# Gated mix of cached attention and a feed-forward layer: K transposed in 32x32 blocks by VectorE, K and V in 64 KB pages, TensorE's program as loops

## The chip, the cores and the metric

One core of one Trainium2 chip runs the whole program. The metric is the device time of one execution in microseconds (us); the time of a version is the median of its runs.

## The reference

One token's row `x` (512 numbers) goes through two branches, and a gate mixes them.

```python
g = sigmoid((x * gate_w).sum(-1))
q = x @ wq                                  # 32 heads of 128
scores = q . k_cache * 128 ** -0.5          # 8 groups of K and V, 4 heads each, 32768 positions
a = (softmax(scores) @ v_cache) @ wo        # wo: 4096 x 512
b = (silu(x @ w_gate) * (x @ w_up)) @ w_down   # 1792 wide
out = g * a + (1 - g) * b
```

All tensors are bf16. `k_cache` and `v_cache` are 8 x 32768 x 128 each, 64 MiB; the weights are 13 MiB more. Every number is used once, for four heads in the case of K and V.

## The kernel before

**Layout.** A group's K or V is 8 MiB. SBUF holds five pages of 32 KB per partition: two for K (`PG_K`), two side by side for V (`PG_V`), and one (`PG_X`) for wq at first and wo at the end. `w_gate` and `w_up` lie in the V pages until V's first load; `w_down` has a tensor of its own (`wd`). A K group is loaded in two halves of 32 KB per partition, a V group in one transfer of 64 KB per partition. With `(p r) d -> p (r d)` a partition gets consecutive positions, so every partition reads one run of HBM.

**Scores.** A score is a sum over the 128 numbers of a position, which stand along a partition's row; TensorE sums over partitions. So K has to be transposed. TensorE does it (`emit_fill`, L397): it takes pairs of bf16 as one fp32 word, and multiplies by an identity, into PSUM (`pst`, two buffers). VectorE copies 128x2048 bf16 at a time from PSUM to `ktT` (L606). Then 16 matmuls with 8 columns each (`emit_scores`, L409) use the transposed K as weights and `qcur` as the moving operand: even and odd numbers of each word have a matmul each. A half group has 8 such units. Units of fills run two ahead of the scores (`LAG`).

**Softmax and V.** VectorE takes the maximum of a half's scores (L611), GpSimd the maximum over partitions (L292), ScalarE the negative bias (L504) and eight exponentials with their sums (L513), into `ET`. With `ET` as weights, 64 matmuls of 512 columns (L450) go over V, in four strips of the array (`32 * c`). ScalarE copies the sums out (L525), and the next turn of the loop reduces them (`emit_reduce`, L435); VectorE keeps them in `oT` (L600).

**Order.** Each engine has its own program; semaphores join them. TensorE's loop (L485) has the eight groups as turns: K in two halves, the reduction of the turn before, V. SP issues all loads in one order: wq, x, gate_w, w_gate, w_up, then per group K half, K half, V, then `wd`, and wo in five pieces (`WO_CUTS`). A K load waits until its half page was transposed one group earlier (L301); a V load waits until V of the group before is used up (L311), the first one until the up projection is done.

**The end.** `emit_end` sums the exponentials with a matmul of ones, reduces the last group, multiplies `w_down` (14 rows) and the first 18 rows of wo as one-row matmuls of 512 columns in four strips (L204), then the last rows of wo in pieces of 128 columns (L216) as they land. `part` (L659) joins the strips; L661 copies the result, and L243 stores it.

Of the kernel before, what the change touches and what calls it, by code (L numbers as in the profile page):

```python
# [4 lines left out]

ACT = mybir.ActivationFunctionType
ALU = mybir.AluOpType
# [6 lines left out]
def bass_gated_mix__gqa_block_cached__swiglu_ffn__decode_kernel(  # L14
# [22 lines left out]
    assert H == 32 and G >= 2  # L37
# [3 lines left out]
    R = 128  # L41
    BLK = 128 * R
    NB = S // BLK
    assert S % BLK == 0 and NB == 2
    NT = NB * R
    PAGE = R * DH
    RPU = 8
    UPP = R // (2 * RPU)
    UPG = NB * UPP
    UW = RPU * 128  # L50
    NKT = 4
    NST = 2
    LAG = 2
    STEP = 16
    WOJ = H * DH // 128
    SCALE = float(DH) ** -0.5
    assert UPG == STEP == 4 * HPG and UPP % NKT == 0 and UPP % NST == 0
    assert KC * H * DH <= PAGE and 2 * KC * F <= PAGE and WOJ * NOUT <= PAGE
    WO_CUTS = [0, 8, 18, 26, 30, 32]
    KW = 1  # L60
    WD_CUT = 8
    WIDE = WO_CUTS[KW + 1]
    OC = NOUT // 128

# [4 lines left out]
    assert RQ * HPG <= 32 and RQ * DH == 512  # L69

    PG_K = (0, 1)
    PG_V = 2
    PG_X = 4
    NPG = 5

    with ExitStack() as es:
# [3 lines left out]
        sem_page = [S_(f"s_page{i}") for i in range(3)]  # L80
        sem_q = S_("s_q")
        sem_f = S_("s_f")
        sem_wo = [S_(f"s_wo{i}") for i in range(len(WO_CUTS) - 1)]
        sem_ld_x = S_("s_ld_x")
        sem_ld_wd = S_("s_ld_wd")
        sem_fill = S_("s_fill")
        sem_sc = S_("s_sc")
        sem_v_free = S_("s_v_free")
        sem_cp = S_("s_cp")
        sem_out = S_("s_out")  # L90
        sem_const = S_("s_const")
        sem_pool = S_("s_pool")
        sem_ident = S_("s_ident")
# [5 lines left out]
        sem_pe_S = S_("s_pe_S")  # L99
        sem_pe_O2 = S_("s_pe_O2")  # L100
        sem_pe_sum = S_("s_pe_sum")
# [4 lines left out]
        sem_dve_t1 = S_("s_dve_t1")  # L106
        sem_dve_tT = S_("s_dve_tT")
        sem_pmax = S_("s_pmax")
        sem_dve_esum2 = S_("s_dve_esum2")
        sem_dve_oT1 = S_("s_dve_oT1")  # L110
        sem_dve_oT2 = S_("s_dve_oT2")
        sem_dve_O2 = S_("s_dve_O2")
        sem_dve_oz = S_("s_dve_oz")
        sem_dve_row = S_("s_dve_row")
        sem_psw = S_("s_psw")
        sem_pe_w = S_("s_pe_w")
        sem_dve_w = S_("s_dve_w")
# [3 lines left out]
        sem_ps0 = S_("s_ps0")  # L121
        sem_acc = S_("s_acc")
        sem_red = S_("s_red")
        sem_rc = S_("s_rc")
        sem_exp = S_("s_exp")
        sem_gtot = S_("s_gtot")
        sem_gmax = S_("s_gmax")

# [3 lines left out]
        x_row = T("x_row", [1, D], BF16)  # L132
        gw_row = T("gw_row", [1, D], BF16)
        ones_bf = T("ones_bf", [1, 2], BF16)
        ones_f = T("ones_f", [128, 128], FP32)
        ident = T("ident", [128, 128], BF16)
        ident_f = T("ident_f", [128, 128], FP32)
        perm = T("perm", [128, 2, 128], BF16)
        pmat = T("pmat", [128, 128], BF16)
        xT = T("xT", [128, KC], BF16)  # L140
        gwT = T("gwT", [128, KC], FP32)
# [6 lines left out]
        qblk = T("qblk", [128, (G + 2) * STEP], BF16)  # L148
        qcur = T("qcur", [128, 2, 2 * HPG], BF16)
        sg = T("sg", [128, FC], FP32)  # L150
        t1 = T("t1", [128, FC], FP32)
        tT = T("tT", [128, FC], BF16)
        wd = T("wd", [128, FC, NOUT], BF16)
        page = T("page", [128, NPG, PAGE], BF16)
        ktT = T("ktT", [128, NKT, 2 * UW], BF16)
        ET = T("ET", [128, NT, HPG], BF16)
        pmaxf = T("pmaxf", [128, NB, HPG], FP32)
        pmax = T("pmax", [128, (G + 1) * STEP], FP32)
        gmax = T("gmax", [128, G, HPG], FP32)
        nbias = T("nbias", [128, G, HPG], FP32)  # L160
        esum = T("esum", [128, G, NB, HPG], FP32)
        esum2 = T("esum2", [128, G, HPG], FP32)
        sel5 = T("sel5", [128, SW + 15], FP32)
        sel4 = sel5[:, SW - 1 : SW + 15]
        acc = T("acc", [128, RQ, DH], FP32)
        oT = T("oT", [128, (G + 2) * STEP], FP32)
        rS = T("rS", [128, H], FP32)
        rSg = T("rSg", [128, H], FP32)
        oTs = T("oTs", [128, H], BF16)
        O2a = T("O2a", [128, WOJ], BF16)  # L170
        O2 = T("O2", [128, WOJ], BF16)
        O2z = T("O2z", [128, WOJ - WIDE, SW], BF16)
        part = T("part", [128, NOUT], FP32)
        res_row = T("res_row", [128, 128], BF16)
# [4 lines left out]
        ps_sc = [P(f"ps_sc{i}", [128, 512], FP32) for i in range(NB)]  # L179
        ps_o = P("ps_o", [128, 512], FP32)  # L180
        ps_m = P("ps_m", [128, 512], FP32)
        pst = [P(f"pst{i}", [128, UW], FP32) for i in range(NST)]
        M_X0 = 0
        M_Q0 = 8
# [3 lines left out]
        M_P0 = M_O0 + WOJ  # L188
        assert M_P0 + HPG <= 512

        ps_e = pst[0][:, 0:512]
        ps_c = pst[1][:, 0:512]
        ps_w = pst[0][:, 512:1024]

        v_page = page[:, PG_V : PG_V + NB, :].rearrange("p b e -> p (b e)")
        v_rows = v_page.rearrange("p (r d) -> p r d", d=DH)

        wq_v = page[:, PG_X, 0 : KC * H * DH].rearrange("p (c n) -> p c n", c=KC)
        wgu = page[:, PG_V, 0 : 2 * KC * F].rearrange("p (w c f) -> p w c f", w=2, c=KC)
        wo_v = page[:, PG_X, 0 : WOJ * NOUT].rearrange("p (j n) -> p j n", j=WOJ)  # L200

        def emit_wide(pe, w, vec, j, first, last):
            c = j % NSTRIP
            return pe.matmul(  # L204
                ps_w[32 * c : 32 * c + 1, :],
                vec[:, j : j + 1],
                w[:, j, :],
                start=first,
                stop=last,
                skip_group_check=True,  # L210
            )

# [13 lines left out]
        def emit_wo(pe, k):  # L226
            pe.wait_ge(sem_wo[k], 16)
            for j in range(WO_CUTS[k], WO_CUTS[k + 1]):
                if j < WIDE:
                    ins = emit_wide(pe, wo_v, O2, j, False, j >= WIDE - NSTRIP)  # L230
                else:
                    ins = emit_rows(
                        pe,
                        lambda e: O2[:, j : j + 1] if e else O2z[:, j - WIDE, :],
                        wo_v[:, j, :],
                        False,
                        j == WOJ - 1,
                    )
            return ins
# [8 lines left out]
        with nc.Block("main") as block:  # L248
            @block.gpsimd
            def _(pool):  # L250
                pool.memset(ones_bf[:, :], 1.0).then_inc(sem_const, 1)
                pool.memset(ones_f[:, :], 1.0).then_inc(sem_const, 1)
# [6 lines left out]

                pool.load_library(library_config.all_libraries[1])  # L260
# [12 lines left out]
                pool.memset(ident[:, :], 0.0)  # L273
                pool.memset(ident_f[:, :], 0.0)
                pool.memset(perm[:, :, :], 0.0)
                pool.memset(sel5[:, :], 0.0)
                chain(pool.memset(pmat[:, :], 0.0))
                ones_where(ident[:, :], 0, [[-1, 128]]).then_inc(sem_ident, 1)
                ones_where(ident_f[:, :], 0, [[-1, 128]]).then_inc(sem_ident, 1)
                for e in range(2):  # L280
                    ones_where(perm[:, e, :], -e, [[0, 2], [-2, 64]]).then_inc(sem_ident, 1)
                ones_where(pmat[:, :], 0, [[-1, 32], [-32, 4]]).then_inc(sem_ident, 1)
                for c in range(NSTRIP):
                    chain(ones_where(sel4, -32 * c, [[-1, 16]]))
                pool.sem_inc(sem_ident, 1)
# [4 lines left out]
                for g in range(G):  # L290
                    pool.wait_ge(sem_pmax, STEP * (g + 1))
                    pool.partition_all_reduce(  # L292
                        gmax[:, g, :], pmax[:, g * STEP : g * STEP + HPG], 128, ReduceOp.max
                    ).then_inc(sem_gmax, 1)

            @block.sync
            def _(sp):
                def load_k(g, b):
                    if g:
                        sp.wait_ge(sem_fill, UPG * (g - 1) + UPP * (b + 1))  # L300
                    sp.dma_start(  # L301
                        page[:, PG_K[b], :],
                        A_k_cache[0, g, :, :].rearrange("(p b r) d -> b p (r d)", b=NB, r=R)[b],
                    ).then_inc(sem_page[b], 16)

                def load_v(g):
                    if g:
                        sp.wait_ge(sem_v_free, g)
                    else:
                        sp.wait_ge(sem_pe_h, 1)  # L310
                    sp.dma_start(  # L311
                        v_page, A_v_cache[0, g, :, :].rearrange("(p r) d -> p (r d)", r=NT)
                    ).then_inc(sem_page[NB], 16)

                sp.dma_start(wq_v, A_wq.rearrange("(p c) n -> p c n", c=KC)).then_inc(sem_q, 16)
                sp.dma_start(x_row[0:1, :], A_x[0, :, :]).then_inc(sem_ld_x, 16)
                sp.dma_start(gw_row[0:1, :], gate_w.unsqueeze(0)).then_inc(sem_ld_x, 16)
                for w, src in enumerate((B_w_gate, B_w_up)):
                    sp.dma_start(
                        wgu[:, w, :, :], src.rearrange("(p c) f -> p c f", c=KC)  # L320
                    ).then_inc(sem_f, 16)
                for g in range(G):
                    for b in range(NB):
                        load_k(g, b)
# [369 lines left out]
```

## Time and profile before

| | us |
|---|---|
| median of 3 runs | 350.92 (350.90 to 350.92) |
| the profiled execution, its own time | 350.87 |
| its span (first to last instruction) | 349.6 |
| PE busy, share of the span | 253.9, 73% |
| DVE busy | 176.0, 50% |
| ACT busy | 33.3, 10% |
| POOL busy | 6.9, 2% |
| granted TensorE clock, mean | 0.883 |

In the profile PE is TensorE's matmuls, PEld its weight loads, DVE VectorE, ACT ScalarE, POOL GpSimd, SP the engine that issues the loads. Busy time of an engine is the union of its instructions. A line such as `L606 DVE COPY ktT<-pst ... x128 | 155.4, 1223 | 115.7 <-PE pst L397 108.1` is a group: source line, engine, operation, what it writes and reads, count, then busy us, mean ns of one, then the us in which the engine stood idle before these instructions, and whose end ended that idle time. A line of the waits has the waiter, the one waited for, us in total, times, and the longest. In the chain that ended last each step is what released the step behind it.

### The profile page before, as it was taken

Reading aid. Unit: us, or ns where it says so; the run is one execution under the profiler, and the core shown is the slowest. Engines: PE = TensorE matmul, PEld = TensorE weight load, DVE = VectorE, ACT = ScalarE, POOL = GpSimd, SP = SyncE. Lnnn points to the kernel's source line nnn. Section 1 sums busy time; section 2 is a strip of 40 time slices with the busy share of each in tenths; the row PEclk is TensorE's granted clock in tenths of the full one; section 3 lists DMA queues with packets and bytes.
Section 4 is the critical chain, followed back from the end, with each engine's and each line's share of the span. In section 5 each row is a group of like instructions: output and inputs, shape, how many; then the busy total and the mean of one; then the engine's idle time right before and its main releaser. Section 6 shows DMA issues by size and latency. Waiting matters only on the chain. (4 is left out here: it accounts for less than half of the span.)

```text
span 349.6 us, 8827 instructions
## 1 busy us (share of the span) xinstructions
PE 253.9 (73%) x4005; PEld 215.2 (62%) x4005; DVE 176.0 (50%) x194; ACT 33.3 (10%) x148; POOL 6.9 (2%) x29
## 2 busy tenths in 40 slices
PE   0446986688945995798955994598866994698584
PEld 0446986278914985298914993298725993398531
DVE  0010986068801984068803883078703883098511
ACT  1000001300030003000030003000030003000210
POOL 4000000000000000000000000000000000000000
PEclk9999999599968997689969987889968987899879
DMA  8999999999989999999999999999999998999995
GB/s 322 419 457 418 472 444 386 428 420 465 457 386 431 442 442 412 432 469 405 442 416 439 457 405 424 435 461 435 405 427 435 457 435 386 450 469 420 391 421 240
DMA packets 4772, 148.23 MB, mean 424 GB/s; under 512 B 538, under 2 KB 540, under 8 KB 796
## 3 DMA queue, kind: packets, MB, share of 16 engines
q1 hardware_dynamic: 4760, 148.12, 98.6%
q8 instruction: 6, 0.10, 0.1%
q14 instruction: 2, 0.02, 0.0%
q10 hardware_dynamic: 4, 0.00, 0.0%
HBM read 148.11 MB, written 0.00 MB: 424 GB/s over the span
## 5 line engine op out<-in xcount | busy, mean ns | idle before, releaser
L606 DVE COPY ktT<-pst 128x2048 bf16<-128x2048 bf16 x128 | 155.4, 1223 | 115.7 <-PE pst L397 108.1
L397 PE MATMUL pst<-ident_f,page 128*128 128x128 f32 x1024 | 144.4, 292 | 28.9 <-DMA page<-in_A_k_cache_dram 24.8
L397 PEld LDWEIGHTS pst<-ident_f,page 128*128 128x128 f32 x1024 | 120.9, 150 | 35.2 <-DMA page<-in_A_k_cache_dram 28.4
L409 PE MATMUL ps_sc<-qcur,ktT 128*128 128x8 bf16 x2048 | 67.6, 166 | 9.0 <-DVE ktT L606 8.0
L409 PEld LDWEIGHTS ps_sc<-qcur,ktT 128*128 128x128 bf16 x2048 | 66.5, 96 | 11.5 <-DVE ktT L606 9.4
L450 PE MATMUL ps_o<-page,ET 128*16 128x512 bf16 x512 | 45.1, 529 | 33.8 <-ACT ET L513 24.8
L450 PEld LDWEIGHTS ps_o<-page,ET 128*16 128x16 bf16 x512 | 15.4, 116 | 60.2 <-ACT ET L513 34.5
L513 ACT ACTIVATE ET<-ps_sc,nbias 128x128 bf16<-128x128 f32 x64 | 23.9, 552 | 0.6
L504 ACT ACTIVATE nbias<-gmax 128x4 f32<-128x4 f32 x8 | 1.6, 205 | 229.7 <-POOL gmax L292 229.7
L513 ACT ACTIVATION_READ_ACCUMULATOR ET<-ps_sc,nbias 128x1 f32 x64 | 18.0, 282 | 0.0
L611 DVE TENSOR_REDUCE pmaxf<-ps_sc 128x4 f32<-128x512 f32 x16 | 11.1, 691 | 11.9 <-PE ps_sc L409 11.9
L383 PE MATMUL ps_m<-xT,page 128*128 128x1 bf16 x112 | 6.9, 198 | 4.9 <-DMA page<-in_B_w_up_dram 4.9
L435 PE MATMUL ps_m<-sel,acc 128*128 128x4 f32 x72 | 10.0, 262 | 0.4 <-ACT acc L525 0.4
L383 PEld LDWEIGHTS ps_m<-xT,page 128*128 128x128 bf16 x112 | 6.8, 163 | 5.0 <-DMA page<-in_B_w_up_dram 5.0
L346 PE MATMUL ps_m<-ones_bf,x_row 1*128 1x1 bf16 x4 | 0.3, 173 | 13.1 <-DMA gw_row<-in_gate_w_dram 13.1
L435 PEld LDWEIGHTS ps_m<-sel,acc 128*128 128x128 f32 x72 | 9.4, 204 | 0.5 <-ACT acc L525 0.5
L525 ACT ACTIVATE acc<-ps_o 128x512 f32<-128x512 f32 x8 | 4.8, 597 | 47.3 <-issue 47.3
L292 POOL PARTITION_ALL_REDUCE gmax<-pmax x8 | 3.0, 371 | 311.9 <-DVE pmax L613 311.9
L346 PEld LDWEIGHTS ps_m<-ones_bf,x_row 1*128 1x128 bf16 x4 | 0.2, 116 | 13.1 <-DMA gw_row<-in_gate_w_dram 13.1
L546 DVE CAST xT<-ps_m 128x4 bf16<-128x4 f32 x1 | 0.2, 160 | 12.0 <-PE ps_m L346 12.0
L585 DVE TENSOR_TENSOR t<-sg,ps_m 128x14 f32<-128x14 f32 x1 | 0.2, 169 | 10.7 <-ACT sg L498 10.7
L359 PE MATMUL ps_m<-xT,page 128*128 128x1 bf16 x128 | 3.6, 165 | 0.3 <-DVE gwT L547 0.3
(65 smaller groups left out, 31.0 us busy)
## 6 DMA issues: line engine op xcount, KB each, us to landing
page<-in_A_k_cache_dram SPq DMA_DIRECT2D x16, 4096.0 KB, 27.5
page<-in_A_wq_dram SPq DMA_DIRECT2D x1, 4096.0 KB, 12.5
page<-in_A_wo_dram SPq DMA_DIRECT2D x2, 1024.0 KB, 40.4
page<-in_B_w_gate_dram SPq DMA_DIRECT2D x1, 1792.0 KB, 15.7
page<-in_B_w_up_dram SPq DMA_DIRECT2D x1, 1792.0 KB, 20.6
wd<-in_B_w_down_dram SPq DMA_DIRECT2D x1, 1792.0 KB, 36.1
page<-in_A_wo_dram SPq DMA_DIRECT2D x1, 1280.0 KB, 40.7
page<-in_A_wo_dram SPq DMA_DIRECT2D x1, 512.0 KB, 43.6
```

What stands on the lines that cost most here:

```text
L292: pool.partition_all_reduce(gmax[:, g, :], pmax[:, g * STEP : g * STEP + HPG], 128, ReduceOp.max).then_inc(sem_gmax, 1)
L359: ins = pe.matmul(ps_m[:, M_Q0 + h : M_Q0 + h + 1], wq_v[:, c, h * DH : (h + 1) * DH], xT[:, c : c + 1], start=(c == 0), stop=(c == KC - 1),)
L383: ins = pe.matmul(ps_m[:, base + j : base + j + 1], wgu[:, w, c, :].rearrange("d (p j) -> d j p", j=FC)[:, j, :], xT[:, c : c + 1], start= ...
L397: ins = pe.transpose(pst[u % NST][:, k * 128 : (k + 1) * 128], kv[:, n * 128 : (n + 1) * 128], ident_f[:, :],)
L409: ins = pe.matmul(ps_sc[b][:, col : col + 2 * HPG], kt[:, k, e, :], qcur[:, e, :], start=(e == 0), stop=(e == 1),)
L435: ins = pe.matmul(ps_m[:, M_P0 : M_P0 + HPG], acc[:, q, :], sel4[:, q * HPG : (q + 1) * HPG], start=(q == 0), stop=(q == RQ - 1),)
L450: ins = pe.matmul(ps_o[32 * c : 32 * c + RQ * HPG, :], ET[:, n : n + RQ, :].rearrange("p n h -> p (n h)"), v_rows[:, n : n + RQ, :], start ...
L504: act.activation(nbias[:, g, :], gmax[:, g, :], ACT.Copy, scale=-SCALE).then_inc(sem_nbias, 1)
L513: act.activation(ET[:, b * R : (b + 1) * R, h], sc[:, h, :], ACT.Exp, bias=nbias[:, g, h : h + 1], scale=SCALE, accum_out=esum[:, g, b, h ...
L525: act.activation(acc[:, :, :].rearrange("p q d -> p (q d)"), ps_o[:, :], ACT.Copy).then_inc(sem_acc, STEP)
L606: dve.tensor_copy(ktT[:, u % NKT, :], pst[u % NST][:, :].bitcast(BF16)).then_inc(sem_cp, 1)
L611: dve.tensor_reduce(pmaxf[:, b, :], sc, AX.X, ALU.max).then_inc(sem_pmax, 4)
```

## The change

K and V each come as one transfer per group of 64 KB per partition. SBUF has three pages of 64 KB: K in pages 0 and 1 in turn, V in page 2. wq, `w_gate` and `w_up` lie in page 2 until the first V; `w_down` and wo go to page 0 after the last K that used it.

TensorE no longer transposes K. VectorE does, straight from the page to `slot` (two slots of 2 KB per partition): `dve.transpose` on fp32 words turns every 32x32 block of words, 128x512 words per instruction, 32 instructions per group. A quarter of 32 partitions is transposed by itself, so partition 32 i + b of a slot holds word b of a 32-word stretch of positions of quarter i. `qblk` is laid out to fit: four matmuls (`JE`) per row block, each with 16 columns, 4 heads for each of 4 quarters (before: two matmuls with 8 columns). The sum of matmuls for scores stays 2048. The exponentials come out by quarter (`E`), and ScalarE copies them to `ET` in the order that V's rows have: 16 copies of 32 partitions x 256 per group, after the copy to `acc`.

TensorE's program is written as loops: the q projection (16 turns), gate and up (14), the scores of a group (16 turns of two units), `w_down` (7), and around scores, V and reduction a loop over `G + 2` turns with branches (`hinted`). In turn j stand the scores of group j, V of group j - 1 and its reduction.

```diff
-    R = 128
-    RPU = 8
-    NKT = 4
-    WO_CUTS = [0, 8, 18, 26, 30, 32]
+    RPU = 2
+    SLOTS = 2
+    NPG = 3
+    WO_CUTS = [0, 24, 28, 30, 32]
+    K_PAGES = 2
+    V_PAGE = 2
+    W_PAGE = 2
+    O_PAGE = 0
+    V7_CUTS = [0, 64, 192, 256]
...
             @block.sync
+                def load_k(j):
+                    if j >= K_PAGES:
+                        sp.wait_ge(sem_tr, UNITS * (j - K_PAGES + 1))
+                    cache(A_k_cache, j, j % K_PAGES).then_inc(sem_k[j % K_PAGES], 16)
+                def load_v(j):
+                    if j:
+                        sp.wait_ge(sem_v_done, VTURN * (j + 1))
...
+                load_k(0)
+                for j in range(G - 1):
+                    load_k(j + 1)
+                    load_v(j)
+                sp.wait_ge(sem_tr, UNITS * (G - 1))
+                sp.dma_start(wd_v, ...).then_inc(sem_ld_wd, 16)
+                for k, sem in enumerate(sem_v7):
+                    a, b = V7_CUTS[k], V7_CUTS[k + 1]
+                    sp.wait_ge(sem_v_done, VTURN * (G - 1) + b // (RQ * VB))
+                    cache(A_v_cache, G - 1, V_PAGE, a, b).then_inc(sem, 16)
+                for k in range(len(sem_wo)):
...
             @block.tensor
-                def emit_fill(b, u):
...
+                def emit_s(j):
+                    n0 = pe.compute_val(j * UNITS)
+                    c0 = pe.compute_val((j & 1) * (RB * NS))
+                    with pe.Fori(0, UNITS // SLOTS, 1) as u:
+                        for s in range(SLOTS):
+                            pe.wait_ge(sem_tr, n0 + u * SLOTS + (s + 1))
+                            for r in range(RPU):
+                                for e in range(JE):
+                                    ins = pe.matmul(ps_sc[...], sv[:, s, r, e // 2, e % 2, :],
+                                                    qcur[:, e, :], ...)
+                            ins.then_inc(sem_sc, 1)
+                def emit_v(j):
+                    pe.wait_ge(sem_v, j * 16)
+                    pe.wait_ge(sem_ep, j)
+                    pe.wait_ge(sem_oc, j)
...
+                def emit_reduce(n):
+                    pe.wait_ge(sem_acc, n)
+                    for q in range(RQ):
+                        ins = pe.transpose(ps_o[:, q * 128 : (q + 1) * 128],
+                                           acc[:, q * 128 : (q + 1) * 128], ident_f[:, :])
+                    ins.then_inc(sem_red, 1)
...
+                def emit_wide():
+                    with pe.Fori(0, FC // 2, 1) as n:
+                        for c in range(2):
+                            pe.matmul(ps_w[0:1, :], vec[:, bass.ds(n * 2 + c, 1)], page[...], ...)
...
+                with hinted(pe, "groups", G + 2) as (j, arm):
+                    with pe.If(j < G + 1):
+                        arm()
+                    with pe.If(j < G):
+                        emit_s(j)
+                    with pe.If(j > G):
+                        emit_wide()
+                    with pe.Else():
+                        with pe.If(j > 0):
+                            emit_v(j)
+                        emit_reduce(j + 1)
...
             @block.scalar
+                    act.wait_ge(sem_v_done, j * VTURN + VTURN)
+                    act.activation(acc[:, :], ps_o[:, :], ACT.Copy).then_inc(sem_acc, 1)
+                    act.wait_ge(sem_exp, j * HPG + 3 * HPG)
+                    for g in range(NQ):
+                        for i in range(NQ):
+                            ins = act.activation(ET[QP * i : ..., ...], E[QP * g : ..., ...], ACT.Copy)
+                    ins.then_inc(sem_ep, 1)
...
             @block.vector
-                            dve.tensor_copy(ktT[:, u % NKT, :], pst[u % NST][:, :].bitcast(BF16))
...
+                        for t in range(UNITS):
+                            s = t % SLOTS
+                            dve.wait_ge(sem_sc, n0 + (t + 1))
+                            dve.transpose(slot_f[...], kp[:, :, t * UW : (t + 1) * UW]...)
+                                .then_inc(sem_tr, 1)
+                        dve.wait_ge(sem_sc, n0 + (UNITS + SLOTS))
+                        dve.tensor_reduce(pmax[:, :], ps_sc[...], AX.X, ALU.max).then_inc(sem_pmax, 1)
+                        dve.tensor_copy(qc, qblk[...])
+                        dve.wait_ge(sem_red, i * K_PAGES + (p + 1))
+                        dve.tensor_reduce(oT[...], o_diag, AX.XY, ALU.add).then_inc(sem_oc, 1)
```

The sums of the exponentials are taken over partitions by GpSimd (`partition_all_reduce` of `esum`) in place of TensorE's matmul with ones; some constants are filled by GpSimd in place of VectorE.

## The prediction

> **What bounds the kernel now.** I read the DMA part of the page first, then the chain of work that ended last, then SP's waits.
>
> ```profile
> q1 hardware_dynamic: 4760, 148.12, 98.6%
> ...
> HBM read 148.11 MB, written 0.00 MB: 424 GB/s over the span
> ```
>
> The 16 DMA engines are busy 98.6% of the span: the load of 148 MB is the kernel. The chain's last pieces (start, length, what) say it again:
>
> ```profile
> 303.85 43.69 DMA page<-in_A_wo_dram
> 347.53 0.04 issue
> 347.57 0.32 PE pst L216 x4
> 347.90 0.02 issue
> 347.92 0.29 DVE res_row L661
> ```
>
> The last piece of wo was issued at 303.85 us, long before its turn, and 2.0 us after it lands (347.53) the span ends. SP never runs dry, although it waits for pages:
>
> ```profile
> SPq L301 <- PE pst L397: 176.7, 14, 14.9
> SPq L311 <- PE ps_o L450: 87.4, 7, 14.7
> ```
>
> These waits cost nothing: a K load is issued 27.5 us (median) before it lands and a V load 32.1 us, so a backlog stands in the queue. The trace's landings: two K parts take 9.71 us each, a V group 19.35 us. The work on the engines is hidden under that, so taking it away is worth nothing by itself. What counts is (a) the bytes per second, (b) whether a load is ever issued too late, (c) what remains after the last landing.
>
> **Part 1, the transfers.** The bytes are the same. K goes in 64 KB per partition, as V does now: 19.35 for 19.42 us, 8 x 0.07 = **-0.6 us**. wo in 24, 4, 2, 2 rows takes what it took in five pieces (9.96 us). Six fetches of instructions, 16 KB each, hold one DMA engine 1 us each today; fewer of them is at most 6 us on 16 engines, 0.4 us, left out.
>
> **Part 2, K's transpose moves from TensorE to VectorE.** Gone: 1024 matmuls of L397 and 128 copies of L606, both hidden under DMA now. New: 256 transposes of 128x512 words. The nearest rows (lines of VectorE; busy, mean ns):
>
> ```profile
> L611 DVE TENSOR_REDUCE pmaxf<-ps_sc 128x4 f32<-128x512 f32 x16 | 11.1, 691 | 11.9 <-PE ps_sc L409 11.9
> L600 DVE COPY oT<-ps_m 128x4 f32 (+1 forms) x9 | 1.5, 162 | 1.4 <-PE ps_m L435 1.4
> ...
> L640 DVE STREAM_TRANSPOSE O2a<-oTs 128x32 bf16<-128x32 bf16 x1 | 0.2, 211 | 0.0
> ```
>
> A column costs (691-162)/508 = 1.04 ns, so a transpose of 512 words is 211 + 480 x 1.04 = 0.71 us. Two copies of 1.22 us that waited for nothing took 2.35 us together, so back to back an instruction costs 0.09 less: 0.62. Bounds: a copy of 2048 bf16 costs 0.6 ns per element, which would give 0.50 (0.41 spaced); two cycles per word would give 1.21. I take 0.62, by the row of the same operation.
>
> There are two slots, so transpose t waits until the scores have read slot t-2. That round trip stands in this stretch of the timeline (start, length):
>
> ```profile
> 324.83 2.54 DVE L606 COPY ktT<-pst 128x2048 bf16<-128x2048 bf16 x2
> ...
> 327.42 0.56 PE L409 MATMUL ps_sc<-qcur,ktT 128*128 128x8 bf16 x16 [0.54 <-DVE ktT L606]
> ...
> 328.08 0.69 DVE L611 TENSOR_REDUCE pmaxf<-ps_sc 128x4 f32<-128x512 f32 x1 [0.72 <-PE ps_sc L409]
> ```
>
> From the copy's end (327.37) through 16 matmuls to VectorE's next start is 0.71 us; a unit now has 8 matmuls, at 0.025 us each 0.2 less: 0.51. Two units need 0.71 + 0.51 = 1.22 us, as much as 2 x 0.62. TensorE's new loop has a branch every two units: the loop's edge at L485 took 0.40 us in the trace's records, some 0.1 of it in the round trip. So a unit is about **0.65 us** (0.61 to 0.80: doubled matmul times or an edge of 0.7 us give the upper end), and the scores S of a group take 31 x 0.65 + 0.71 + 0.5 = 21.4 us.
>
> **Part 3, is a load late?** One V page instead of an early fill: V(j+1) may be issued only when V(j) is used up. TensorE does the scores of j+1 and then V(j); VectorE, at a group's end, waits for the reduction that follows V(j-1), and all its transposes of the next group are queued behind that. So one turn is S 21.4 + V 5.4 + acc copy 0.6 (L525) + four transposes 0.8 (L397) + a reduce 0.25 + semaphores 0.2 = 28.7 us, against 38.7 us of DMA per group. In the **middle** nothing is late. ScalarE's 16 new copies per group (each between 0.20, L504, and 0.60, L525: 3 to 10 us) run beside S and are due after it: no cost while they stay under 20 us. The matmul loops at the start (30 edges of 0.4 us more) end near 37 us, and K's first group lands at 42.4: hidden, with 5 us to spare. GpSimd's sums and fills lie beside loads.
>
> **At the start:** scores of group 0 from 42.4 to 63.9; then maximum (1.22), GpSimd and bias (0.8), four exponentials (2.1), acc, transposes, reduce: 6 us; scores of group 1 from 69.9 to 91.3; V(0) until 95 to 97; V(1)'s first packet 1 us later (the first load took 0.74 to 1.74). K(2) fills DMA until 100. Hidden with 2 us to spare: it is lost from a unit of 0.69 us on, with 64 us per us of unit.
>
> **At the end** the cover is thin. SP's order is K7, V6, wd (4.3 us), V7 in three parts, wo. The first part of V7 waits for the first 64 rows of V6 to be used, and wo is queued behind it. K7 lands at x; scores until x + 21.5 (V6 landed at x + 19.35); 16 matmuls, the semaphore, SP and first packet: x + 23.7 to 24.6. wd's packets end at x + 23.1. **+1.0 us** (0.6 to 1.5), growing 32 us per us of unit.
>
> **Part 4, after the last landing.** Today wo lands after V by 14 us, which hides V, sums and wd. Now V7's last part is followed only by wo, 9.95 us; from its landing T to the end of the last matmuls that DMA alone would allow is T + 10.3. The chain: 16 matmuls, 1.1 to 2.0; acc 0.65; four transposes 0.7 to 1.05; branches 0.2; 14 matmuls of wd, now all in one strip, so one after the other, 14 x 0.216 = 3.0 (4.7 with the first eight at 0.427); O2 0.6; then 24 wide matmuls not before wo's first piece (T + 7.5) 1.5; copy of part 0.75 (L659); rows 0.45 + 0.65. It ends at T + 10.8 to 12.2: **+0.5 to +1.9**, I take 1.2.
>
> The spread is TensorE's clock, seen in the two stretches of one V stage (the last three columns: granted clock, DMA share, GB/s):
>
> ```profile
> 97.60:104.30 6.70, 3.59 (x36) 1.34 (x40) 0.00 (x0) 2.54 (x16) 0.00 (x0) 0.50 0.91 391
> 104.40:110.00 5.60, 1.72 (x32) 0.59 (x24) 0.00 (x0) 0.60 (x1) 0.00 (x0) 1.00 1.06 456
> ```
>
> Four matmuls side by side took 0.427 us at clock 0.5 and 0.216 at 1.0. [...]
>
> **Sum**, against the profiled execution: span 349.6 - 0.6 + 1.0 + 1.2 = 351.2; its own time, 350.87, is 1.27 over its span: 352.5. The median of the runs is 350.92, the same within 0.05. **Forecast 352.5 us**, +0.45%.
>
> **Rivals.**
> 1. *Nothing is late.* If VectorE keeps 0.61 us per unit and the clock stays at 1.0, the gap at the end is 0.2 or nothing and the tail 0.4 or less: 349.6 - 0.6 + 0.0 to 0.6 + 1.27 = 350.3 to 350.9, not slower. For it: the 2 us of margin everywhere else, and a clock of 1.0 in half of the windows. Against: wd in one strip. It decides below a unit of 0.62.
> 2. *The round trip is the pace.* At 0.80 us per unit, start and end both starve: (0.80 - 0.69) x 64 = 7.0, and 1.0 + 0.15 x 32 = 5.8: 349.0 + 12.8 + 1.2 + 1.27 = 364. For it: only two slots, a branch per two units. Against: the 0.51 us of the trace.
> 3. *Words transpose at half rate*: 1.21 us, S 39.6, a turn of 47 us beats DMA's 38.7 in all groups: the first V is used up at about 133 us, the sixth after at 133 + 6 x 47 = 415, then V7 19.4, wo 10, 2: about 445. The only transpose in the trace is of bf16.
> 4. *TensorE's code is not at hand.* The final branch to the second block waits for a 16 KB fetch (in the trace's records 1 us to a first packet, 1 us of packet, 0.5 us to landing): 2.5 us in the tail, 355.0. [...] The trace's branch at L485 shows no such stall (0.40 us).
>
> That K's path stays on TensorE is ruled out: no instruction of L397 is left.
>
> **How the numbers follow.** Forecast (with gaps of 0.5 to 4 us in all) 0.44; rival 4 0.03; rival 1 0.25; rival 2 and units between 0.69 and 0.85 0.22; rival 3 0.06. Range 350.2 to 362: it leaves out rival 3, the top of 2, and the lowest part of 1. A difference of 0.2% (350.2 to 351.6) is about what this measurement can tell from none. Faster, 0.12, is half of rival 1, with fewer fetches beside; same, 0.23, its other half and the forecast's low edge; slower, 0.65, the rest. The forecast's own range is 351 to 355.
>
> **What would show it.** Transposes near 0.71 us each, spaced 0.65; DMA share again near 0.98 with its only dips at V7's first part; V7's first issue after wd's end by a us; the last matmuls 1 us behind wo's landing. A K group that lands later than 19.35 us after the load before it, anywhere in the middle, would make the prediction wrong, as would transposes over 0.9 us.

## The result and the profile after

379.85 us is the median (379.57 to 381.08, 4 runs) against 350.92 before in the same runs: a ratio of 1.083 (95% interval 1.081 to 1.086). The forecast was 352.5, in a range to 362. The profiled execution of the changed kernel has a span of 379.6 us, 30.0 more than before.

The page after, its row of DMA by slices of the span, its queue and its rate:

```profile
DMA  8999997987903999999999999999989999978993
...
q1 hardware_dynamic: 3752, 148.12, 91.2%
q8 instruction: 1, 0.02, 0.0%
...
HBM read 148.11 MB, written 0.00 MB: 390 GB/s over the span
```

The bytes are the same; the 16 DMA engines are busy 91.2% of the span instead of 98.6%. The row says where not: from the seventh to the thirteenth slice (57 to 123 us; the zero alone is 9.5 us without a transfer) and from the 36th on (332 us). In between nearly all is 9. SP's waits say on whom the loads waited:

```profile
SPq L314 <- PE ps_o L446: 256.6, 9, 39.4
SPq L314 <- PE ps_m L399: 56.8, 1, 56.8
...
SPq L314 <- DVE slot L625: 22.8, 1, 22.8
```

Before, SP's waits for pages came to 290 us (336 now) and cost nothing, since a backlog stood in the queue. Now one wait of 56.8 us, for the up projection (`ps_m`, L399), holds V(0) until 60.6 us. Before, the same load left SP at 29.74, after this wait:

```profile
SPq L311 <- PE ps_m L383: 26.0, 1, 26.0
```

The landings (when a load's last part has arrived, by the semaphore) give the loss at each place, as the time from one landing to the next beyond the usual 19.35 us:

| load | landed after (us) | late by |
|---|---|---|
| K(0), K(1) | 40.96, 60.31 | 0 |
| V(0) | 83.01 | 3.35 |
| K(2) | 105.54 | 3.18 |
| V(1) | 142.71 | 17.81 |
| K(3) to V(6), `w_down` | 340.69 | 0.2 in all |
| V(7) in three parts | 364.53 | 4.48 |
| wo, last piece | 374.42 | 0 |
| end of the span | 379.6 | 5.2 behind wo, before 2.0: 3.2 |

Together 32.2. Some came back: K takes 0.31 less in the first group and 7 x 0.08 after it, and 1.17 at the start, where the up projection lands at 21.61 instead of 22.78. That leaves 30.2 for the 30.0 by which the span grew.

The timeline of the changed kernel shows what the first wait waits for (start, length, what):

```profile
57.91 1.14 PE L399 MATMUL ps_m<-xT,page 128*128 128x1 bf16 x8 [0.40 <-issue]
...
59.44 1.14 PE L399 MATMUL ps_m<-xT,page 128*128 128x1 bf16 x8 [0.40 <-issue]
60.62 0.33 SPq L314 DMA_DIRECT2D page<-in_A_v_cache_dram  x1
...
61.71 1.30 DVE L625 STREAM_TRANSPOSE slot<-page 128x512 f32<-128x512 f32 x2 [0.36 <-issue]
```

A turn of the gate and up loop takes 1.54 us for 8 matmuls of one column, and idle time is put down to "issue": TensorE waits for nothing but its own program. The last turn ends at 60.6, and both V(0)'s load and the first transpose of K, whose page had landed at 40.96, stand behind it. The prediction had these loops end near 37.

**Theory A**: these loops, slow by themselves, delay V(0), K(2) and V(1); the rest is a unit of scores (0.69 us) that is too long for the start and the end. **Rivals**: B, the new score stage alone (round trip, softmax) makes the loads late, and the start matters little; C, TensorE's code comes too late. C has little for it: the queue of instructions (q8) has a single packet of 16 KB in the whole profile, at 375.65 us; besides, q14 has one of 8 KB, at 79.30.

### The profile page after: what moved, and what is told of

Its sections match the earlier page's. It is cut to its first block, busy times and chain, and to the rows that moved or that the text cites. A ratio compares the mean times of both kernels' runs of the same rounds, so it can differ in the third digit from the quotient of the medians.

```text
span 379.6 us, 8401 instructions
## 1 busy us (share of the span) xinstructions
PE 200.8 (53%) x2923; PEld 132.3 (35%) x2923; DVE 185.4 (49%) x304; ACT 92.5 (24%) x220; POOL 8.6 (2%) x32
## 3 DMA queue, kind: packets, MB, share of 16 engines
q1 hardware_dynamic: 3752, 148.12, 91.2%
## 5 line engine op out<-in xcount | busy, mean ns | idle before, releaser
L625 DVE STREAM_TRANSPOSE slot<-page 128x512 f32<-128x512 f32 x256 | 167.0, 690 | 49.9 <-DMA page<-in_A_k_cache_dram 39.5
L422 PE MATMUL ps_sc<-qcur,slot 128*128 128x16 bf16 x2048 | 104.3, 179 | 120.4 <-DVE slot L625 106.8
L422 PEld LDWEIGHTS ps_sc<-qcur,slot 128*128 128x128 bf16 x2048 | 81.5, 107 | 144.3 <-issue 143.2
L545 ACT ACTIVATE ET<-E 32x256 bf16<-32x256 bf16 x128 | 52.8, 412 | 1.4
L532 ACT ACTIVATE E<-ps_sc,nbias 128x256 bf16 x32 | 21.8, 853 | 1.8 <-ACT nbias L527 1.8
L376 PE MATMUL ps_m<-xT,page 128*128 128x1 bf16 x128 | 17.7, 183 | 7.5 <-issue 6.7
L399 PE MATMUL ps_m<-xT,page 128*128 128x1 bf16 x112 | 16.0, 214 | 5.3 <-issue 5.2
L376 PEld LDWEIGHTS ps_m<-xT,page 128*128 x128 | 13.3, 104 | 11.9 <-issue 8.8
L399 PEld LDWEIGHTS ps_m<-xT,page 128*128 x112 | 14.6, 138 | 6.6 <-issue 6.1
L460 PE MATMUL ps_o<-ident_f,acc 128*128 128x128 f32 x36 | 6.8, 319 | 11.0 <-ACT acc L541 10.3
L634 DVE TENSOR_REDUCE pmax<-ps_sc 128x4 f32<-128x1024 f32 x8 | 9.8, 1225 | 4.8 <-PE ps_sc L422 4.8
L527 ACT ACT_TABLE_LOAD x8 | 10.3, 1283 | 0.1
L460 PEld LDWEIGHTS ps_o<-ident_f,acc 128*128 128x128 f32 x36 | 4.4, 157 | 15.5 <-ACT acc L541 13.9
L600 DVE TENSOR_TENSOR sg<-sg,ps_m 128x14 f32<-128x14 f32 x1 | 0.2, 171 | 19.4 <-ACT sg L517 19.4
## 6 DMA issues: line engine op xcount, KB each, us to landing
page<-in_B_w_up_dram SPq DMA_DIRECT2D x1, 1792.0 KB, 19.4
```

Of the source, the lines that this page charges most:

```text
L376: ins = pe.matmul(ps_m[:, bass.ds(h * 2 + (M_Q0 + e), 1)], wq_v[:, c, bass.ds(h * (2 * DH) + e * DH, DH)], xT[:, c : c + 1], start=(c == 0 ...
L399: ins = pe.matmul(ps_m[:, bass.ds(f + base, 1)], wgu[:, w, c, :].rearrange("d (p j) -> d j p", j=FC)[:, bass.ds(f, 1), :].rearrange("d j p ...
L422: ins = pe.matmul(ps_sc[:, bass.ds(c0 + u * (SLOTS * RPU * NS) + (s * RPU + r) * NS, NS),], sv[:, s, r, e // 2, e % 2, :], qcur[:, e, :], ...
L460: ins = pe.transpose(ps_o[:, q * 128 : (q + 1) * 128], acc[:, q * 128 : (q + 1) * 128], ident_f[:, :],)
L527: act.activation(nbias[:, :], gmax[:, :], ACT.Copy, scale=-SCALE).then_inc(sem_nbias, 1)
L532: act.activation(ev[:, h, :, :], scv[:, h, :, :], ACT.Exp, bias=nbias[:, h : h + 1], scale=SCALE, accum_out=esum[:, bass.ds(j * HPG + h, 1 ...
```

## The experiments

**1. The start written out.** The changed kernel with both loops at the start as plain instructions with constant addresses; nothing else differs.

```diff
-with pe.Fori(0, FC, 1) as f:
+for f in range(FC):
     for w, base in enumerate((M_G0, M_U0)):
         for c in range(KC):
             ins = pe.matmul(
-                ps_m[:, bass.ds(f + base, 1)],
+                ps_m[:, base + f : base + f + 1],
...
```

> The changed kernel with the q projection and gate/up written out (128 and 112 matmuls with constant addresses) and no other edit. Theory A: the two loops at the start are the loss; they end at 60.6 us, so group 0's scores start at 61.7 although K landed at 41.0, and the first V and the next K and V land 3.4, 3.2 and 17.8 us late. Written out, scores start at 41; with 0.69 us per unit the second V's load still starts 3.8 us after DMA has run dry: about 20.5 us gained, 359. Theory B: the start only moves work, and the pace is the turn of one V page and two slots: the loss stays, 372 or more.

360.45 us, 1.026 of before (1.023 to 1.030): 19.4 of the 28.9 us are back. V(0) and K(2) land on time, V(1) 3.75 late instead of 17.81. The two projections in the list of groups, first the changed kernel:

```profile
L376 PE MATMUL ps_m<-xT,page 128*128 128x1 bf16 x128 | 17.7, 183 | 7.5 <-issue 6.7
L399 PE MATMUL ps_m<-xT,page 128*128 128x1 bf16 x112 | 16.0, 214 | 5.3 <-issue 5.2
```

and written out:

```profile
L399 PE MATMUL ps_m<-xT,page 128*128 128x1 bf16 x112 | 6.9, 198 | 4.7 <-DMA page<-in_B_w_up_dram 4.7
...
L375 PE MATMUL ps_m<-xT,page 128*128 128x1 bf16 x128 | 3.6, 165 | 0.5 <-DVE prod_col L568 0.5
```

One matmul lasts nearly as long (165 and 183 ns, 198 and 214); what grows is the busy union, 3.6 to 17.7 and 6.9 to 16.0, since in the loops they hardly overlap. Idle time at the edges adds 6.7 and 5.2. Theory A holds, and B keeps the rest.

**2. The same loops in long turns.** q in 4 turns of 32 matmuls, gate and up in 2 of 56; each matmul still computes its address from the loop's register.

```diff
-with pe.Fori(0, H // 2, 1) as h:
-    for e in range(2):
+with pe.Fori(0, H // 8, 1) as h:
+    for e in range(8):
...
-with pe.Fori(0, FC, 1) as f:
+with pe.Fori(0, 2, 1) as f:
+    for f7 in range(FC // 2):
```

> The changed kernel with the same loops at the start in longer turns: q in 4 turns of 32 matmuls (was 16 of 8), gate/up in 2 turns of 56 (was 14 of 8). If the turn's edge were the cost (as the prediction had it, with dense matmuls between), the loops would end near 31 us and the time would be as with the loops written out, 359. If each matmul whose address comes from a register costs 0.124 us, as the distance of neighbours in the profile says, q takes 128 x 0.124 + 4 x 0.57 = 18 us and gate/up 112 x 0.124 + 2 x 0.57 = 15 us: they end near 48 us and the time is about 366.

369.27 us, 1.051 (1.046 to 1.056): 3 us above the second of the two cases expected, with the loops ending at 50.4 instead of near 48. q takes 19.0 us instead of 24.4, gate and up 16.2 instead of 21.2. Two equations for each, matmuls times m plus turns times t (128 m + 16 t = 24.4, 128 m + 4 t = 19.0; 112 m + 14 t = 21.2, 112 m + 2 t = 16.2), give m = 0.134 and 0.137, t = 0.45 and 0.42. Before, a matmul cost 3.58 / 128 = 0.028 and 6.88 / 112 = 0.061:

```profile
L383 PE MATMUL ps_m<-xT,page 128*128 128x1 bf16 x112 | 6.9, 198 | 4.9 <-DMA page<-in_B_w_up_dram 4.9
...
L359 PE MATMUL ps_m<-xT,page 128*128 128x1 bf16 x128 | 3.6, 165 | 0.3 <-DVE gwT L547 0.3
```

So an edge costs what the prediction gave it; the matmuls cost 2 to 5 times what it left unchanged. The records have a register instruction (FUSED_REGOPS, 46 ns) ahead of each.

**3. Only the loops, in the kernel before.** The two loops of the change, put into the kernel before, with the counts that the others wait for; its scores, V and pages are untouched.

```diff
-for h in range(H):
+with pe.Fori(0, H // 2, 1) as h:
+    for e in range(2):
...
```

> The kernel before with only the two loops of the start taken over (q in 16 turns, gate/up in 14), all else as it was. Theory A: gate/up end near 60 us, the first V load is issued then instead of at 29.7, and DMA, which holds K until 42, stands still for some 19 us: about 370. Theory B, that loops are cheap and the pages are the loss: 351 to 355.

375.22 us, 1.068 (1.063 to 1.073): 24.3 us more, from two loops alone. Its row of DMA:

```profile
DMA  8999205999999999999999999999999999999893
```

One hole, at 37 to 65 us, and 9 from there to 346 us: V(0) leaves SP at 60.43, lands at 83.98, 43.03 behind K(0) instead of 19.35. Nothing that is lost there comes back, since DMA has no slack (98.6% busy before). The loss in the loads is the 19.5 us between K(0)'s landing (40.95) and the issue, and 4.2 that the load took beyond 19.35; 1.5 came back, since K(0) had landed at 42.44 before. That is 22.2 us, by which wo lands later (369.70 instead of 347.53). The other 2.1 us stand behind that landing: the span ends 4.1 us after it instead of 2.0. TensorE needs 6.6 us for V(7) there, before 5.1, and its granted clock in that stretch is 0.55, before 0.70; why is open.

**4. Four slots.** The changed kernel with four slots for transposed K in place of two (the copy of sums shares `ET`'s place to make room, and its next filling waits for the reduction).

```diff
-    SLOTS = 2
+    SLOTS = 4
...
-        acc = T("acc", [128, RQ * DH], FP32)
+        acc = ET[:, :].bitcast(FP32)
...
+                    act.wait_ge(sem_red, j + 1)
```

> The changed kernel with four slots instead of two (to make room, the copy of the sums lies where the permuted exponentials lie, and ScalarE waits for the reduction before it writes them). If the round trip to TensorE and back sets the pace, a unit falls from 0.69 to the 0.64 us that two transposes without a wait are apart, S by 1.65 us, which counts twice at the start and once at the end: 375. If transposes cannot follow each other faster, 380.

370.66 us, 1.055 (1.050 to 1.059): 9.2 below the changed kernel, more than expected. VectorE in the first group's scores, the changed kernel:

```profile
61.71 22.07 DVE L625 STREAM_TRANSPOSE slot<-page 128x512 f32<-128x512 f32 x32 [0.36 <-issue]
84.36 1.23 DVE L634 TENSOR_REDUCE pmax<-ps_sc 128x4 f32<-128x1024 f32 x1 [0.58 <-PE ps_sc L422]
...
90.91 0.23 DVE L647 TENSOR_REDUCE oT<-ps_o 128x64 f32 x1 [5.24 <-PE ps_o L460]
91.13 2.08 DVE L625 STREAM_TRANSPOSE slot<-page 128x512 f32<-128x512 f32 x3
```

and with four slots:

```profile
61.30 19.10 DVE L626 STREAM_TRANSPOSE slot<-page 128x512 f32<-128x512 f32 x32 [0.36 <-issue]
```

32 transposes without a break, 0.69 us apart before and (19.10 - 0.67) / 31 = 0.595 after. So with two slots the round trip was the pace after all. In the changed kernel the starts are by turns 0.64 and 0.71 to 0.80 us apart: every second transpose waits. The first pair's round trip, from a transpose's end (62.42) over its scores to the start of the next but one (63.06), took 0.64 us. The edit also makes TensorE's loop 8 turns of four units in place of 16 of two; what the longer turns alone give was not measured. The lines below the first show the pause between two groups: from 83.78 to 91.13 VectorE has the maximum and then waits 5.24 us for the chain over GpSimd, ScalarE and TensorE. A single transpose lasts longer than the spacing with four slots: 0.67 us (mean of 256) against 0.595. V(1) is 12.5 us late instead of 17.8, K(2) 1.4 instead of 3.2, V(7) 1.2 instead of 4.5.

**5. `w_down` in four strips, written out**, as before the change.

```diff
-                    with pe.Fori(0, FC // 2, 1) as n:
-                        for c in range(2):
-                            pe.matmul(
-                                ps_w[0:1, :],
...
+                    for n in range(FC):
+                        c = n % NSTRIP
+                        pe.matmul(
+                            ps_w[32 * c : 32 * c + 1, :],
...
```

> The changed kernel with the 14 matmuls of w_down written out and spread over four strips of the array instead of a loop in one strip. Theory: in the changed kernel these 14 stand on the path behind the last reduction (368.8 to 374.0 us at half clock) and the 24 wide matmuls of wo behind them; spread, they end near 370.5, the wide ones start when wo's first piece has landed (371.9), and the end comes 2.6 us earlier: 377.2. Rival: the end is set by the landing of wo or by fetching the code behind the block: 379.9.

378.92 us (378.18 and 379.65), 1.079 (1.074 to 1.083): 1 us or less. The tail of the changed kernel on TensorE:

```profile
368.80 4.54 PE L473 MATMUL ps_w<-page,vec 128*1 x12 [0.53 <-issue]
373.51 0.59 PE L473 MATMUL ps_w<-page,vec 128*1 x2 [0.17 <-issue]
374.04 0.19 PE L482 MATMUL ps_m<-O2a,pmat 128*128 128x32 bf16 x1
374.51 1.47 PE L489 MATMUL ps_w<-page,vec 128*1 128x512 bf16 x24 [0.28 <-DVE vec L661]
```

and in strips:

```profile
366.84 1.87 PE L473 MATMUL ps_w<-page,vec 128*1 128x512 bf16 x14 [0.20 <-issue]
368.65 0.21 PE L482 MATMUL ps_m<-O2a,pmat 128*128 128x32 bf16 x1
371.19 2.73 PE L489 MATMUL ps_w<-page,vec 128*1 128x512 bf16 x24 [2.33 <-DMA page<-in_A_wo_dram]
```

The loop took 5.3 us, the strips 1.87, as meant. But now the wide matmuls wait 2.33 us for wo's first piece, and take 2.73 instead of 1.47. The windows of both tails give the granted clock (start and end, length, busy us of the engines, then clock, DMA share, GB/s); first the changed kernel, `w_down` and the wide matmuls:

```profile
368.80:374.10 5.30, 5.13 (x15) 1.19 (x15) 0.25 (x2) 0.00 (x0) 0.00 (x0) 0.69 0.85 346
374.50:376.00 1.50, 1.47 (x24) 0.48 (x24) 0.05 (x1) 0.00 (x0) 0.00 (x0) 1.00 0.06 11
```

then the strips, the pause, the wide matmuls:

```profile
366.80:368.70 1.90, 1.86 (x15) 0.46 (x15) 0.58 (x3) 0.00 (x0) 0.00 (x0) 0.50 1.08 466
368.90:371.10 2.20, 0.00 (x0) 0.00 (x0) 0.28 (x2) 0.00 (x0) 0.00 (x0) 0.50 0.75 315
371.20:373.90 2.70, 2.70 (x24) 0.64 (x24) 0.00 (x0) 0.00 (x0) 0.00 (x0) 0.50 0.71 270
```

During the slow loop the granted clock went from 0.50 (368.8 to 372.1 us) to 1.00 (from 372.2), and the wide matmuls ran at 1.00; from the short strips to the end of the wide matmuls it stayed at 0.50. No run shows what raised it. The mean granted clock of the changed kernel is 0.72, before 0.883.

**6. The three together** (1, 4 and 5).

> The three edits together: start written out, four slots, w_down in four strips. With the start written out the second V is issued 3.8 us late; four slots bring each group's scores 2.9 us earlier, twice over, so this gap goes; V7's gap at the end falls from 4.1 to about 1.2; the tail falls by some 2.3. Sum 360.45 - 3.8 - 2.9 - 2.3 = 351.4. If one of the three covered the other (a common cause), it would be 354 or more.

353.23 us, 1.005 (1.003 to 1.008); the profiled execution took 352.67, its span 351.4. The sum of the spans' gains alone would be 20.5 + 10.3 + 1.4 = 32.2; it is 28.2, since 1 and 4 both recover the same lateness of K(2) and V(1). All loads up to V(6) land 19.35 us apart. What is left stands at the end: V(7) 1.2 late, and 3.3 us from wo's last landing to the end.

**7. V's last group in four parts.** 6, with a first part of 32 rows, so that it waits for less of V(6).

```diff
-    V7_CUTS = [0, 64, 192, 256]
+    V7_CUTS = [0, 32, 96, 192, 256]
```

> The three edits and V7 in four parts, the first of 32 rows (cuts 0, 32, 96, 192, 256), so that its first part waits for 8 matmuls of V6 instead of 16. If V7's remaining gap is the wait for those matmuls at half clock, 0.85 us less than the three edits alone: 350.5, the same as the kernel before within 0.2%. If the gap is issue and first packet only, no difference.

354.36 us (351.62 to 356.28, 12 runs), 1.007 (1.005 to 1.010): nothing gained, and a scatter of almost 5 us. The profiled execution is the slowest of the twelve. In it V(7)'s four parts land 22.7 us behind `w_down`; the wide matmuls take 2.73 there, as at a granted clock of 0.50 in experiment 5, and 1.53 in the profile of 6.

**8. Only q written out**: 7, but gate and up again as the loop (what was expected of it speaks of V(7) in three parts; it has 7's four).

> As the three edits (V7 in three parts), but only q is written out and gate/up stay a loop of 14 turns. The loop would end at 22 + 14 x 1.54 = 43.5 us, and group 0's scores start at 44.5 instead of 42.7; with less code the fetch that delays up's landing by 1.2 us may go. Late by 1.8 at the start where four slots leave 2 us, early by 1.2 in DMA: within 1 us of the three edits. If the head has no spare, 1.8 us more.

354.77 us, 1.011 (1.008 to 1.015), no more than 7 within their scatter. V(0) leaves at 44.76 instead of 30; its queue had work until 61.8, so 15 us later is still early enough for V(0). V(1) is 1.34 late.

**9, 10, 11. Wo's first piece.** Two experiments had left the tail at over 3 us. In the profile of 6 the wide matmuls start behind the landing of wo's first piece of 24 rows, 2.5 us ahead of the last. Before, 18 rows had gone that way, in two pieces. Experiment 9 is 6 with

```diff
-    WO_CUTS = [0, 24, 28, 30, 32]
+    WO_CUTS = [0, 16, 24, 28, 30, 32]
```

> The version with the start written out, four slots and w_down in strips, and besides wo loaded in pieces of 16, 8, 4, 2, 2 rows instead of 24, 4, 2, 2 (16 wide matmuls, the other rows in pieces of 128 columns). In the version without this edit the 24 wide matmuls started right behind the landing of wo's first piece (345.5 of a span of 351.4), 2.5 us before the last piece, and what follows them (1.5 us, 1.07 to the rows, the rows, the copy, the store) ends 3.3 us behind the last landing instead of 2.0. Theory A (the first piece of wo is too long for the cover behind it): 16 rows land about 2.5 us earlier, the end is about 2.0 us behind the last landing again, span near 350.1, 351.4 by time (353.2 to 351.9 by medians), and the scatter shrinks, since a wide stage at half clock is covered too. Theory B (TensorE's clock alone sets the tail): 32 more short matmuls beside it leave the time at 353 or above.

10 adds the cuts of 7, 11 leaves `w_down` as the loop.

> The version before, and V's last group in four parts, the first of 32 rows instead of 64. The gap in the loads ahead of the last V group was 1.1 us with the cut at 64 rows, because the first part waits for the first 64 rows of the group before to be used. If the gap is the time of the second eight matmuls, it shrinks to about 0.4 us: 0.7 us below the version without this edit (350.7 to 351.2). If it moves to the second part, as in the one profile of this cut so far, no difference.

> As the first of these, but w_down left as the loop of one strip. In the changed kernel that loop took 5.3 us where four strips take 1.9; with wo's first piece 2.5 us earlier nothing covers it: O2 comes 3.4 us later than in the version in strips, the wide matmuls start some 2.5 to 3 us behind that piece: 1 to 2 us slower than the version in strips, 352.5 to 354 by the median. If w_down is still covered, no difference between the two.

9 took 351.76 us (1.0023, interval 1.0004 to 1.0043; profiled execution 351.57), 10 took 353.38 (1.004, 1.002 to 1.006), 11 took 354.68 (1.009, 1.006 to 1.011). TensorE in the tail of 9:

```profile
342.02 1.87 PE L471 MATMUL ps_w<-page,vec 128*1 128x512 bf16 x14
...
343.82 0.21 PE L480 MATMUL ps_m<-O2a,pmat 128*128 128x32 bf16 x1
...
344.32 1.28 PE L487 MATMUL ps_w<-page,vec 128*1 128x512 bf16 x16 [0.28 <-DVE vec L660]
```

The wide matmuls no longer wait for a landing (wo's first piece came at 343.03) but for their operand, and end 2.5 us ahead of wo's last landing at 348.13; the span ends 2.0 behind that, as before the change. Theory A's 351.4 by time and 351.9 by medians stand beside 351.57 and 351.76, though the clock of the wide stage is still 0.78:

```profile
344.30:345.60 1.30, 1.28 (x16) 0.33 (x16) 0.10 (x1) 0.00 (x0) 0.00 (x0) 0.78 0.92 381
```

The tail was set by the order of the pieces, and not by the clock alone. The queue of 9 is as full as the one of the kernel before:

```profile
q1 hardware_dynamic: 3896, 148.12, 98.3%
```

In 11 the loop over `w_down` ends at 348.0, 0.4 us ahead of wo's last landing, and the time is 2.9 above 9 (expected 1 to 2). In 10 the first part's packets begin before `w_down`'s have ended (316.68 and 317.34 us), so the gap is gone where it was, but the four parts together land 2.46 us late instead of 1.22 in 9. With the same four parts it was 3.37 in the profile of 7 and 0.87 in that of 8, so one profile of each version doesn't tell what smaller parts do to V(7). By the medians they cost 1.1 us (7 against 6) and 1.6 (10 against 9); why stays open.

No version is faster than before. The best, 9, lies 0.2% above it.

## Why the prediction was wrong

The direction was right, the size was not: 28.9 us instead of 1.6.

- **The step that failed** is "The matmul loops at the start (30 edges of 0.4 us more) end near 37 us, and K's first group lands at 42.4: hidden, with 5 us to spare". The edges were right (0.42 to 0.45, experiment 2). The term left at zero was the matmuls': 128 x (0.134 - 0.028) + 112 x (0.137 - 0.061) = 22 us, since each has its address computed from a register. The loops end at 60.6. Experiment 3 shows that this step alone costs the kernel before 24.3 us, 22.2 of them in its loads; experiment 1 that in the changed kernel it is 19.4, after 1.25 us that go to a fetch of instructions (19.36 us, 16 KB) beside its written-out start: the up projection lands at 22.86 instead of 21.61. The trace of before had no matmul with an address from a register. For the transpose, which that trace did not have either, the prediction worked out bounds; for this cost it gave none.
- **Restarting the queue** was taken as "V(1)'s first packet 1 us later". The first packet did come 0.96 us after each issue (V(0), K(2), V(1), V(7)). But from issue to landing it took 22.4 us for V(0) and 22.0 for V(1), 2.7 to 3.0 over the 19.35 of a load in a full queue. The page of before had that number: wq's 4 MiB landed 12.5 us after its issue, where a K part takes 9.7.
- **The unit of scores** was 0.69 us, not 0.65. A transpose lasted as forecast (690 ns against 0.71) and can follow another after 0.595 (forecast 0.62), but the round trip with two slots was longer than 0.51. Rival 2 is therefore partly true: "The round trip is the pace", at 0.69 and not 0.80. The start was said to lose from 0.69 on; in experiment 1, where the unit alone is left, V(1) is 3.75 late and V(7) 4.1. Beside the unit stand a softmax of 7.4 us between two groups' scores (taken as 6) and the restart.
- **V(7)'s gap** was given 1.0, with 32 us per us of unit: 1.0 + 0.04 x 32 = 2.3 by the unit measured. It was 4.5. Its first part landed 7.3 us after the issue, 2.4 over the 4.84 that as many rows take in a full queue; the 1.4 above the assumed 1 us is most of the rest.
- **The tail** was given 1.2 (0.5 to 1.9) and lost 3.2. `w_down` in one strip took 5.3 us, 3.0 was taken: half clock at first (the first nine matmuls start 0.38 to 0.43 us apart, until 372.2), then edges (0.38 and 0.55 from a turn's second matmul to the next turn's first, 0.216 within a turn). Experiments 5 and 9 show that two edits were needed to get it back, the strips and an earlier first piece of wo.
- **Right**: K in 64 KB parts takes 19.35 us (0.08 saved in each of seven groups; of the 0.31 in the first, 0.23 may be a fetch at 30.70 in the kernel before, since experiment 1, with one at 30.84, has K(0) 0.23 late); between K(3) and V(6) nothing is late; ScalarE's copies are hidden (6.8 us per group); VectorE does not transpose words at half rate (0.69 us, not 1.21: rival 3 is out); no code fetch stops TensorE (rival 4 is out: the branch to the last block lies before 368.8, the only fetch of 16 KB at 375.65).

## What to carry to other kernels

The matmuls of one column here cost 0.028 us with a constant address and 0.134 with one from a register: ask of every small instruction that moves into a loop whether its address is still a constant, and price the register arithmetic per instruction, not only the loop's edge. Where DMA is the bound, as here, a hole in its queue was not made up later, and it cost the idle time plus 2.4 to 4.2 us of restart: list for each load by how much its issue precedes the end of the queue's work, and price the load by a row that was issued to an empty queue. In a tail, follow each piece to the last landing: a faster stage gained 1 us or less here until the piece that it waited for came earlier too.

## What the runs showed of the hardware that was not expected

- Matmuls of one column with an address from a register mostly start 0.124 us apart within a turn of 8 (0.134 and 0.137 on average, by experiment 2), against 0.028 and 0.061 with constant addresses. The edge of a loop is 0.42 to 0.45 us, of which the records show a compare and branch of 0.21. That cost came with no fetch of instructions in these loops: they end at 60.6 us, and the changed kernel's one fetch of 16 KB is at 375.65.
- The restarts here took 2.4 to 4.2 us over the transfer (V(7)'s first part, and V(0) in experiment 3).
- In the eight versions with a fetch of 16 KB of instructions at 18.9 to 19.6 us, beside a full queue, the up projection landed 5.27 to 5.81 us behind the gate's; in the five without one, 4.28 to 4.31. The packet of such a fetch takes 1.0 us of one of 16 engines, and the landing moved by 1.0 to 1.5. Other fetches moved the next landing by nothing (33.15 us in experiment 6) to 1.3 us (K(1) in experiment 2, with one at 42.71).
